# Two layers of attention and feed-forward on one core: score slots of three and two PSUM banks, with two banks shared by side work and single VectorE tiles

## The chip, the cores and the metric

The kernel runs on one core of one Trainium2 chip. The metric is the device time of the kernel in microseconds (us), from its first to its last instruction; the four executions of each kernel here lie within 0.4% of each other. The time before is 1714 us.

Names of engines: PE is TensorE (PEld its weight loads), ACT is ScalarE, DVE is VectorE, POOL is GpSimd, SP issues most transfers. PSUM is the memory in which TensorE leaves its results; it has eight banks, and one 128 x 512 fp32 result fills a bank.

## The reference

Two layers, each attention with 32 heads of width 16 over 2048 rows, then a gated feed-forward.

```python
def _A_ref(x, wqkv, wo):                 # x: 1 x 2048 x 512
    B, S, D = x.shape; H = 32; Dh = D // H
    qkv = ...(x @ wqkv)...               # cut: split into q, k, v by head
    scores = jnp.einsum("bhqd,bhkd->bhqk", q, k) * (Dh ** -0.5)
    p = _softmax(scores, axis=-1)
    o = jnp.einsum("bhqk,bhkd->bhqd", p, v)
    return ...(o)... @ wo
def _B_ref(x, w_gate, w_up, w_down):     # inner width 1792
    return (_gelu(x @ w_gate) * (x @ w_up)) @ w_down

x = A_x                                  # everything below twice, same weights
x = x + _A_ref(_layernorm(x), A_wqkv, A_wo)
x = x + _B_ref(_layernorm(x), B_w_gate, B_w_up, B_w_down)
```

Per layer there are 32 heads x 2048 x 2048 scores. In tiles of 128 keys x 512 queries that makes 2048 tiles a layer, 4096 in all. Each tile needs a matmul of contraction 16 (padded to 32 rows of the array), an exponential of every element, and a matmul with the values.

## The kernel before

The program is built by a list scheduler that runs while the kernel is being built. It keeps a clock of its own, decides the order of every engine's instructions, and emits a static program with semaphores. So a small edit of its rules changes the order of thousands of instructions.

The eight PSUM banks before: bank 7 collects attention outputs; banks 0 to 2 and 3 to 5 are two *slots* for scores; bank 6 is the only bank for *side work* (projections, the attention output projection, the feed-forward, transposes). A slot is filled by one burst of up to three score matmuls on different row groups of the array, and emptied by one ScalarE exponential.

```python
free_banks = set(range(7))               # 0-5 become the slots when scores start; 6 stays
...
def slot_banks():
    b0 = 3 * (slot_no[0] % 2)
    return [b0, b0 + 1, b0 + 2]
```

VectorE takes part of the exponentials. It adds a constant to the scaled score, clamps at zero and writes an int16, whose bits read as fp16 are about the exponential. Three further copies, shifted by quarters of an octave, are made on VectorE from a group of four such tiles, and the four variants are averaged by the value matmuls. In the kernel before, VectorE gets the *third* tile of a slot, and the choice is made for a group of 12 tiles (four slots) at once:

```python
size = 3 if m is not None and not pace["haste"] else 2
d = size == 3 and started_all() and vector_group() and behind() < LAG
for i in range(0, n, size):
    cur.append((layer, u, part, tiles, 4 * m + i // 3 if d else None, ...))
...
na = n - (dslot is not None)             # tiles that ScalarE takes from this slot: 2 or 3
o = sch.op("act", lambda e: e.activation(PT[...], PS[:, b0:b0 + na, :], ACTF.Exp, scale=...), ...)
...
slot_open[si] += 1                       # the slot can't be refilled before VectorE has drained it
dve(0, [(lambda e: e.tensor_scalar(PI[...], bank(b0 + n - 1), DBIAS, 0.0,
                                   op0=ALU.add, op1=ALU.max), ...)], then)
```

When TensorE would be idle for long, the scheduler inserts filler matmuls that add zero to bank 7. They are meant to keep TensorE's clock up. Near the end of a layer there is a hurried stretch ("haste"), in which scores go without VectorE and two banks of the slots are lent to side work.

## Time and profile before

| | before |
|---|---|
| median | 1714.07 us (1712.64 to 1716.61, 3 runs) |
| ScalarE busy | 1562 us, of it exponentials 1489 us |
| exponentials | 1092 of two banks, 348 of three |
| VectorE score tiles | 868 of 4096 |
| ScalarE idle before exponentials | 79 us |

From the page of the kernel before: its first line, the busy time of each engine, and the shares of the chain of waits by engine.

```profile
span 1715.0 us, 38081 instructions
...
PE 1614.4 (94%) x16017; PEld 489.6 (29%) x16017; DVE 1377.6 (80%) x2287; ACT 1562.4 (91%) x1486; POOL 201.0 (12%) x217
...
ACT 51%; PE 37%; DVE 9%; issue 1%; SPq 1%; DMA 1%; POOL 0%; DVEq 0%; POOLq 0%
```

ScalarE is at 91% over the whole span, and in the stretch with exponentials it is nearer 95%. The chain gives ScalarE half and TensorE over a third, so the two nearly tie.

The page's group of all exponentials. The numbers after the bar are the busy time in us and the mean of one in ns; then the idle time of ScalarE just before them, and what ended most of it.

```profile
L1149 ACT ACTIVATE fPT<-fPS 128x1024 bf16<-128x1024 f32 (+1 forms) x1440 | 1488.7, 1181 | 79.3 <-PE fPS L1144 76.9
```

So 1489 us are work and 79 us are waits for score matmuls. The groups of the kernel before with different shapes kept apart, in the same columns:

```profile
L1149 ACT ACTIVATE fPT<-fPS 128x1024 bf16<-128x1024 f32 x1092 | 1033.6, 1075 | 45.6 <-PE fPS L1144 43.9
L1183 DVE TENSOR_SCALAR fPI<-fPS 128x512 int16<-128x512 f32 x868 | 569.6, 682 | 92.2 <-PE fPS L1144 90.2
L1144 PE MATMUL fPS<-fQ,fKT 32*128 32x512 bf16 x4096 | 550.4, 386 | 62.4 <-ACT fPT L1149 45.1 <-DVE fPI L1183 5.2 <-DVE fQ L634 2.0
L1149 ACT ACTIVATE fPT<-fPS 128x1536 bf16<-128x1536 f32 x348 | 482.4, 1513 | 33.7 <-PE fPS L1144 33.1
L1274 PE MATMUL fPS<-fONB,fZV 128*17 128x512 bf16 x2724 | 212.0, 388 | 3.0 <-POOL fQMASK L361 1.5 <-DVE fOS L827 1.5
```

The first and fourth lines are the two kinds of exponentials, the second VectorE's score tiles, the third the score matmuls, the last the filler.

ScalarE's waits for score matmuls in four windows of the kernel before, in this order: 20 to 131 us, 131 to 790, 790 to 990 (around the layer boundary), 990 to 1680. The numbers are us in total, how many, and the longest.

```profile
ACT fPT L1149 <- PE fPS L1144: 17.1, 4, 6.6
ACT fPT L1149 <- PE fPS L1144: 17.6, 41, 1.9
ACT fPT L1149 <- PE fPS L1144: 20.1, 21, 11.4
ACT fPT L1149 <- PE fPS L1144: 18.2, 40, 1.7
```

With the 3.9 us before the first exponential these make the group's 76.9 us. In the first window it is four waits, in the third one of 11.4 us and twenty short ones; the other two consist of short waits only, 0.4 us on average. ScalarE's timeline of the kernel before, cut to the long gaps and the end (start in us, length, then the instructions; in brackets the idle time before):

```profile
17.39 12.21 ACT L1149 ACTIVATE fPT<-fPS 128x1536 bf16<-128x1536 f32 x9 [3.90 <-PE fPS L1144]
32.47 6.82 ACT L1149 ACTIVATE fPT<-fPS 128x1536 bf16<-128x1536 f32 x5 [2.87 <-PE fPS L1144]
41.44 31.87 ACT L1149 ACTIVATE fPT<-fPS 128x1536 bf16<-128x1536 f32 x30 [2.14 <-PE fPS L1144]
79.88 43.85 ACT L1149 ACTIVATE fPT<-fPS 128x1024 bf16<-128x1024 f32 x44 [6.58 <-PE fPS L1144]
129.26 1.45 ACT L1149 ACTIVATE fPT<-fPS 128x1536 bf16<-128x1536 f32 x1 [5.52 <-PE fPS L1144]
...
841.60 13.84 ACT L1149 ACTIVATE fPT<-fPS 128x1536 bf16<-128x1536 f32 x14 [11.35 <-PE fPS L1144]
...
1639.76 3.82 ACT L1149 ACTIVATE fPT<-fPS 128x1024 bf16<-128x1024 f32 x4 [0.68 <-PE fPS L1144]
1674.58 1.28 ACT L917 ACT_TABLE_LOAD   x1 [31.00 <-PE fPS L590]
```

From the last exponential's end (1639.76 + 3.82 = 1643.58 us) to the end of the span are 71.4 us, in which ScalarE has nearly nothing to do.

TensorE waits for VectorE's score tiles before score bursts, as matmul and as weight load (us in total, how many, and the longest):

```profile
PE fPS L1144 <- DVE fPI L1183: 5.2, 16, 0.9
PEld fPS L1144 <- DVE fPI L1183: 3.7, 10, 0.5
```

These 8.9 us are little.

### The profile page before, as it was taken

The page shows a single profiled execution, that of the slowest core. Times are in us where ns is not written, and L with a number is a line of the kernel's source. Part 1 is how long each engine was busy: PE and PEld are TensorE (multiplying, and loading weights), DVE is VectorE, ACT ScalarE, POOL GpSimd, SP SyncE. Part 2 cuts the span into 40 slices and gives each one's busy share as a digit, 9 for nine tenths or more (in the row PEclk, how much of TensorE's full clock was granted, in tenths as well). Part 3 has the DMA queues.
Part 4 walks back from the last instruction along what each step waited for, and adds up shares of the span by engine and source line. Part 5 has one row for each costly group of instructions (what it writes and reads, how often), then busy time and mean ns, then how long its engine had stood idle before and what let it go on. Part 6 is the DMA issues. An engine that isn't in the chain of part 4 may idle for free.

```text
span 1715.0 us, 38081 instructions
## 1 busy us (share of the span) xinstructions
PE 1614.4 (94%) x16017; PEld 489.6 (29%) x16017; DVE 1377.6 (80%) x2287; ACT 1562.4 (91%) x1486; POOL 201.0 (12%) x217
## 2 busy tenths in 40 slices
PE   8999989999999999999999999999999999999998
PEld 3333222222222222332333222222222222222233
DVE  7788868888898889878743878988888888887953
ACT  5889999999999999999699999999999999999932
POOL 2313011100211021000420110101011100201000
PEclk9999989999999999999999999999999999999999
DMA  4100000224202241125314000012330124112523
GB/s 136 51 2 18 2 18 20 53 76 141 51 27 56 88 145 37 40 53 160 92 47 145 26 18 10 16 40 59 118 110 26 54 70 142 49 38 61 151 59 107
DMA packets 140289, 111.88 MB, mean 65 GB/s; under 512 B 13904, under 2 KB 129872, under 8 KB 140112
## 3 DMA queue, kind: packets, MB, share of 16 engines
q1 hardware_dynamic: 136416, 104.78, 21.4%
q0 software_dynamic: 2112, 4.19, 0.9%
q8 instruction: 130, 2.13, 0.5%
q10 hardware_dynamic: 1584, 0.39, 0.1%
q14 instruction: 47, 0.39, 0.1%
HBM read 97.78 MB, written 6.82 MB: 61 GB/s over the span
## 4 chain that ended last, share of the span: by engine, by line
ACT 51%; PE 37%; DVE 9%; issue 1%; SPq 1%; DMA 1%; POOL 0%; DVEq 0%; POOLq 0%
ACT fPT L1149 50%; PE fPS L590 12%; PE fPS L1144 9%; PE fPS L1254 8%; PE fPS L1274 4%; DVE fPP L1205 4%; DVE fPI L1183 3%; PE fPS L951 2%; ACT fHT L1115 1%; PE fPS L654 1%; DVE fQ L634 1%; SPq L276 1%; DVE fHT L937 1%; PE fPS L567 0%; ACT L1115 0%
## 5 line engine op out<-in xcount | busy, mean ns | idle before, releaser
L1149 ACT ACTIVATE fPT<-fPS 128x1024 bf16<-128x1024 f32 (+1 forms) x1440 | 1488.7, 1181 | 79.3 <-PE fPS L1144 76.9
L1183 DVE TENSOR_SCALAR fPI<-fPS 128x512 int16<-128x512 f32 x868 | 569.6, 682 | 92.2 <-PE fPS L1144 90.2
L1144 PE MATMUL fPS<-fQ,fKT 32*128 32x512 bf16 x4096 | 550.4, 386 | 62.4 <-ACT fPT L1149 45.1
L1205 DVE TENSOR_SCALAR fPP<-fPI 128x2048 int16<-128x2048 int16 x651 | 442.2, 716 | 5.9 <-PE fPS L1254 3.7
L1254 PE MATMUL fPS<-fPT,fVP 128*17 128x512 bf16 x3228 | 438.2, 386 | 6.8 <-DVE fPP L1205 2.6
L1254 PE MATMUL fPS<-fPP,fVD 128*17 128x512 f16 x2604 | 334.1, 381 | 10.7 <-DVE fPP L1205 9.8
L1144 PEld LDWEIGHTS fPS<-fQ,fKT 32*128 32x128 bf16 x4096 | 139.0, 91 | 593.4 <-ACT fPT L1149 491.3
L1254 PE MATMUL fPS<-fPI,fVP 128*17 128x512 f16 x868 | 241.7, 385 | 1.7 <-DVE fPP L1205 1.6
L590 PE MATMUL fPS<-fXNT,fWR 128*128 128x512 bf16 x896 | 226.7, 381 | 5.3 <-DVE fHT L937 4.9
L1274 PE MATMUL fPS<-fONB,fZV 128*17 128x512 bf16 x2724 | 212.0, 388 | 3.0 <-POOL fQMASK L361 1.5
L1254 PEld LDWEIGHTS fPS<-fPT,fVP 128*17 128x17 f16 x3228 | 98.8, 87 | 162.4 <-issue 114.2
L937 DVE TENSOR_TENSOR fHT<-fPS,fHT 128x512 bf16<-128x512 f32 x112 | 76.7, 687 | 68.3 <-PE fPS L590 55.1
L786 POOL TENSOR_TENSOR fAT<-fOS,fRB 128x512 bf16<-128x512 f32 x32 | 42.3, 1322 | 715.9 <-DMA fRB<-rscr 567.4
L951 PE MATMUL fPS<-fWR,fHT 128*128 128x512 bf16 x448 | 123.4, 383 | 0.5 <-DVE fQ L634 0.4
L1254 PEld LDWEIGHTS fPS<-fPP,fVD 128*17 128x17 f16 x2604 | 78.8, 88 | 102.4 <-issue 43.4
L590 PEld LDWEIGHTS fPS<-fXNT,fWR 128*128 128x128 bf16 x896 | 71.9, 97 | 121.1 <-DVE fHT L937 21.2
L914 DVE CAST fHT<-fPS 128x512 bf16<-128x512 f32 x98 | 67.1, 686 | 39.7 <-PE fPS L590 39.7
L1274 PEld LDWEIGHTS fPS<-fONB,fZV 128*17 128x17 f16 x2724 | 61.7, 91 | 68.5 <-issue 33.0
L667 POOL TENSOR_SCALAR fVD<-fVP 128x544 f16<-128x544 f16 (+1 forms) x48 | 53.8, 1124 | 152.5 <-DVE fVP L675 149.9
L546 POOL TENSOR_SCALAR fLNS<-fMV 128x4 f32<-128x4 f32 (+1 forms) x17 | 5.8, 342 | 517.9 <-DVE fMV L539 517.9
L1254 PEld LDWEIGHTS fPS<-fPI,fVP 128*17 128x17 f16 x868 | 51.4, 87 | 40.6 <-issue 22.1
L827 DVE COPY fOS<-fPS 128x512 f32<-128x512 f32 x64 | 43.7, 682 | 15.1 <-PE fPS L1254 14.9
(60 smaller groups left out, 697.5 us busy)
## 6 DMA issues: line engine op xcount, KB each, us to landing
fWR<-in_B_w_down_dram SPq DMA_DIRECT2D x189, 256.0 KB, 3.0
fWR<-in_B_w_gate_dram SPq DMA_DIRECT2D x56, 256.0 KB, 3.3
fWR<-in_B_w_up_dram SPq DMA_DIRECT2D x56, 256.0 KB, 2.9
fRB<-rscr SPq DMA_DIRECT2D x256, 32.0 KB, 1.9
fX<-in_A_x_dram POOLq DMA_DIRECT2D x4, 1024.0 KB, 6.0
xscr<-fX SPq DMA_DIRECT2D x16, 256.0 KB, 2.6
fX<-xscr SPq DMA_DIRECT2D x4, 1024.0 KB, 6.0
fAT<-fATS SPq DMA_DIRECT2D x128, 16.0 KB, 1.8
```

The source lines that it names most:

```text
L590: ins = e.matmul(bank(bs[0])[:, 0:cols], lhsT=l, rhs=r_, start=(i == 0), stop=(i == n - 1))
L667: job("pool", 2, [(lambda e, dst=dst, src=src, ph=ph: e.tensor_scalar(dst, src, 2.0 ** (-ph / NPH), None, op0=ALU.mult), [("VP", c, k) for ...
L827: fn = lambda e: e.tensor_copy(OS[:, s, :], bank(ACC))
L914: evac_job(1, b, [(lambda e: e.tensor_copy(HT[:, ft, :], bank(b)), [BK[b]], [("HT", ft)], 0.6)], got(("gate", layer, qb, ft)))
L937: (lambda e: e.tensor_tensor(HT[:, ft, :], bank(b), HT[:, ft, :], op=ALU.mult), [BK[b], ("HT", ft)], [("HT", ft)], 0.62)], got(("up", laye ...
L951: ins = e.matmul(bank(b)[:, 0:D], lhsT=HT[:, ft, i * 128:(i + 1) * 128], rhs=WR[:, s, jj * D:(jj + 1) * D], start=(ft == 0), stop=(ft == N ...
L1144: ins = e.matmul(bank(b0 + k), lhsT=KT[32 * j:32 * j + 32, c, kt * 128:(kt + 1) * 128], rhs=Q[32 * j:32 * j + 32, qs, :], start=True, stop ...
L1149: o = sch.op("act", lambda e: e.activation(PT[:, p, 0:512 * na].rearrange("p (a b) -> p a b", a=na), PS[:, b0:b0 + na, :], ACTF.Exp, scale ...
L1183: dve(0, [(lambda e: e.tensor_scalar(PI[:, gi, 512 * r:512 * (r + 1)], bank(b0 + n - 1), DBIAS, 0.0, op0=ALU.add, op1=ALU.max), [bks[-1]], ...
L1205: shifts.append((s, [(lambda e: e.tensor_scalar(PP[:, s, :], PI[:, gi, :], int(OCT) * ph // NPH, None, op0=ALU.add), [("PI", gi, r) for r ...
L1254: ins = e.matmul(PS[32 * j:32 * j + VW, ACC, :], lhsT=l, rhs=r_, start=a, stop=z, tile_position=(0, 32 * j), skip_group_check=True)
L1274: ins = e.matmul(PS[32 * j:32 * j + VW, ACC, :], lhsT=ZV[:, :], rhs=ones, start=False, stop=False, tile_position=(0, 32 * j), skip_group_c ...
```

## The change

The intent: give side work and VectorE two banks in common, and let ScalarE have its slots alone. The slots become three banks (0 to 2) and two banks (3 and 4); banks 5 and 6 are shared. VectorE now takes single tiles, each in a shared bank, whenever its backlog allows, from the next few tiles in the queue. A burst may be held back until a shared bank comes free, as long as ScalarE has 0.45 us of work left. The normalised rows, Q, K and the attention rows become fp16 instead of bf16. The core of the diff, with cuts:

```diff
+    WAIT_D = 0.45
...
-    XNT = sb("fXNT", [128, NCK, S], BF)
-    KT = sb("fKT", [128, NCK, S], BF)
+    XNT = sb("fXNT", [128, NCK, S], F16)
+    KT = sb("fKT", [128, NCK, S], F16)
...                      # likewise Q, AT, ATS, the identity and the ones
+    SLOTS = ((0, 1, 2), (3, 4))
...
     def slot_banks():
-        b0 = 3 * (slot_no[0] % 2)
-        return [b0, b0 + 1, b0 + 2]
+        return list(SLOTS[slot_no[0] % 2])
...
+    def vector_bank():
+        if not free_banks:
+            return None
+        return min(free_banks, key=lambda b: (sch.ready("pe", w=[BK[b]]), b))
...
+    def pick(look=False):
+        cap = slot_cap()
+        want_d = not look and started_all() and behind() < LAG and vector_tile()
+        bd = vector_bank() if want_d else None
+        if bd is None or sch.ready("pe", w=[BK[bd]]) > now[0] + 0.02:
+            want_d = False
+        ...                # up to cap tiles for ScalarE and at most one for VectorE
...
+        if started_all() and not pace["haste"] and (free_banks or vb_busy):
+            free = min(...)                      # when the first shared bank comes free
+            if ready < free <= sch.free["act"] - WAIT_D:
+                ready = free
...
-    free_banks.update(range(6))
+    free_banks.update(range(5))
```

The shifted copies may now be made for fewer than four tiles where a unit ends. Smaller edits of the same diff: in the hurried stretch a burst may fill its whole slot (two tiles before) and one bank of a slot is lent instead of two, and value matmuls are also hurried when shifted copies wait for a buffer.

More of the change, by code (lines that the diff above doesn't have):

```diff
@@ L224, in _emit_fast @@
     HT = sb("fHT", [128, NFT, 512], BF)
-    IDN = sb("fIDN", [128, 128], BF)
-    ONB = sb("fONB", [128, 128], BF)
+    IDN = sb("fIDN", [128, 128], F16)
+    ONB = sb("fONB", [128, 128], F16)
     CM05 = sb("fCM05", [128, 4], F32)
@@ L236, in _emit_fast @@
     NQS = 6
-    Q = sb("fQ", [128, NQS, 512], BF)
+    Q = sb("fQ", [128, NQS, 512], F16)
     NOS = HB + 4
@@ L242, in _emit_fast @@
     RB = sb("fRB", [128, NRB, 512], F32)
-    AT = sb("fAT", [128, NCK, 512], BF)
-    ATS = sb("fATS", [128, 2, 512], BF)
+    AT = sb("fAT", [128, NCK, 512], F16)
+    ATS = sb("fATS", [128, 2, 512], F16)
     ST = sb("fST", [128, 8, 6], F32)
@@ L266, in bankbf @@
     def bankbf(b):
-        return PS[:, b, :].bitcast(BF)
+        return PS[:, b, :].bitcast(F16)
     wire = [0.0]
@@ L483, in give_back @@
             lent.discard(b)
-            slot_open[b // 3] -= 1
+            slot_open[0 if b in SLOTS[0] else 1] -= 1
         elif b in held3:
@@ L496, in piece_banks @@
                 if not slot_open[s]:
-                    pool_.update(range(3 * s, 3 * s + 3))
-        if pace["haste"] and slot_no[0] >= 2 and not returned[0]:
-            pool_.update(3 * s + 2 for s in range(2) if not slot_open[s])
+                    pool_.update(SLOTS[s])
+        if pace["haste"] and slot_no[0] >= 2 and not returned[0] and not slot_open[0]:
+            pool_.add(2)
         pool_ -= held3
@@ L515, in emit_piece @@
                     free_banks.discard(b)
-                elif b % 3 == 2 and pace["haste"]:
+                elif b == 2 and pace["haste"]:
                     held3.add(b)
                 else:
-                    slot_open[b // 3] += 1
+                    slot_open[0 if b in SLOTS[0] else 1] += 1
                     lent.add(b)
@@ L531, in xn @@
     def xn(i, alt):
-        return HT[:, i + 4 * alt, 0:D]
+        return HT[:, i + 4 * alt, 0:D].bitcast(F16)
     def xnkey(i, alt):
@@ L964, in post @@
                 if last:
-                    ob = XNT[:, i % NCK, 512 * qb + (i // NCK) * D:512 * qb + (i // NCK) * D + D]
+                    ob = XNT[:, i % NCK, 512 * qb + (i // NCK) * D:512 * qb + (i // NCK) * D + D].bitcast(BF)
                     def store(o, i=i, tt=tt, ob=ob):
@@ L1016, in _emit_fast @@
     DBIAS = OCT * (15.0 - LOG2_4M)
-    groups = []
+    segs = []
     for layer in range(n_rep):
         us = list(range(NU))
-        def unit(u, part, m0, m1, rest):
-            for m in range(m0, m1):
-                groups.append((layer, u, part, 12 * m, 12, m, m == m1 - 1 and not rest))
-            if rest:
-                groups.append((layer, u, part, 12 * m1, 4 * NKT - 12 * m1, None, True))
         if NQB > 1:
-            np_, m = (NPART, NMA) if layer else (2, 1)
+            np_, kts = (NPART, NKT - 4) if layer else (2, 4)
             for u in us[:np_]:
-                unit(u, "A", 0, m, False)
+                segs.append((layer, u, "A", 0, 4 * kts))
             for u in us[:np_]:
-                unit(u, "B", m, NM, 4 * NKT > 12 * NM)
+                segs.append((layer, u, "B", 4 * kts, 4 * NKT))
             us = us[np_:]
         for u in us:
-            unit(u, "F", 0, NM, 4 * NKT > 12 * NM)
+            segs.append((layer, u, "F", 0, 4 * NKT))
     cur = []
@@ L1042, in _emit_fast @@
     pt_no = [0]
-    dg_no = [0]
+    dg = {"n": 0, "items": [], "uk": None, "done": [0]}
     pp_no = [0]
@@ L1049, in _emit_fast @@
     started = {}
+    seg_left = {}
     closed = set()
@@ L1053, in slot_banks, with slot_cap, vector_tile @@
     def slot_banks():
-        b0 = 3 * (slot_no[0] % 2)
-        return [b0, b0 + 1, b0 + 2]
-    def vector_group():
-        if pend.get(("PI", dg_no[0] % NPI)):
+        return list(SLOTS[slot_no[0] % 2])
+    def slot_cap():
+        bs = slot_banks()
+        return len([b for b in bs if b not in held3])
+    def vector_tile():
+        if pace["haste"]:
+            return False
+        if not dg["items"] and pend.get(("PI", dg["n"] % NPI)):
             return False
@@ L1063, in vector_group @@
         return late < DVE_LATE
+    def vector_bank():
+        if not free_banks:
+            return None
+        return min(free_banks, key=lambda b: (sch.ready("pe", w=[BK[b]]), b))
+    vb_busy = {}
     def take_slot():
@@ L1068, in take_slot, with pull, tile_keys @@
         slot_no[0] += 1
+    def pick(look=False):
[4 more added lines that the diff above has]
+            want_d = False
+        a, d = [], None
+        for x in cur:
+            if len(a) == cap and (d is not None or not want_d):
+                break
+            t = x[3]
+            if want_d and d is None and t % 3 == 2 and t < 12 * NM and (not dg["items"] or dg["uk"] == x[:3]):
+                if len(a) == cap or all(y[3] % 4 != t % 4 for y in a):
+                    d = x
+                    continue
+            if len(a) < cap:
+                a.append(x)
+            elif x[3] > a[-1][3] + 3 or x[:3] != a[-1][:3]:
+                break
+        return a, d
+    def pull():
+        while len(cur) < 6 and nxt[0] < len(segs):
+            layer, u, part, t0, t1 = segs[nxt[0]]
+            if (layer, "q", u // 2) not in have or (layer, "k", (u % NG) // 2, t0 // 16) not in have:
+                break
+            nxt[0] += 1
+            uk = (layer, u, part)
+            seg_left[uk] = t1 - t0
+            cur.extend((layer, u, part, t) for t in range(t0, t1))
+    def tile_keys(x):
+        layer, u, part, t = x
+        c = (u % NG) // 2
+        return [("Q", (layer * NU + u) % NQS), ("KT", c, t // 16)]
     def fill_ready():
@@ L1076, in fill_ready @@
             return None
-        e = next_slot()
-        if e is None:
-            return None
-        layer, u, part, tiles, ds, _ = e
-        c = (u % NG) // 2
-        if (layer, "q", u // 2) not in have:
-            return None
-        for kb in {t // 16 for t in tiles}:
-            if (layer, "k", c, kb) not in have:
-                return None
-        if pend.get(("PT", pt_no[0] % NPT)) or len(tiles) == 3 and 3 * s + 2 in held3:
-            return None
-        return sch.ready("pe", [("Q", (layer * NU + u) % NQS)] + [("KT", c, kb) for kb in {t // 16 for t in tiles}],
-                         [BK[b] for b in slot_banks()[:len(tiles)]])
@@ L1092, in left @@
-    def left():
-        return cur or nxt[0] < len(groups)
-    def next_slot():
-        if not cur and nxt[0] < len(groups):
-            layer, u, part, t0, n, m, end = groups[nxt[0]]
-            if (layer, "q", u // 2) not in have or (layer, "k", (u % NG) // 2, t0 // 16) not in have:
-                return None
-            nxt[0] += 1
-            size = 3 if m is not None and not pace["haste"] else 2
-            d = size == 3 and started_all() and vector_group() and behind() < LAG
-            for i in range(0, n, size):
-                tiles = list(range(t0 + i, t0 + min(i + size, n)))
-                cur.append((layer, u, part, tiles, 4 * m + i // 3 if d else None, end and i + size >= n))
-        return cur[0] if cur else None
@@ L1108, in fill @@
-    def fill():
-        a_slot(cur.pop(0))
+        pull()
+        a, _ = pick(True)
+        a = [x for x in a if (x[0], "k", (x[1] % NG) // 2, x[3] // 16) in have]
+        if not a:
+            return None
+        if pend.get(("PT", pt_no[0] % NPT)):
+            return None
+        keys = []
+        for x in a:
+            keys += tile_keys(x)
+        ready = sch.ready("pe", keys, [BK[b] for b in slot_banks()[:len(a)]])
+        if started_all() and not pace["haste"] and (free_banks or vb_busy):
+            free = min([sch.ready("pe", w=[BK[b]]) for b in free_banks]
+                       + [max(sch.free["dve"], now[0]) + 0.75 for b in vb_busy])
+            if ready < free <= sch.free["act"] - WAIT_D:
+                ready = free
@@ L1111, in _emit_fast @@
+        return ready
+    def left():
+        return cur or nxt[0] < len(segs)
+    def fill():
+        a, d = pick()
+        ok = lambda x: (x[0], "k", (x[1] % NG) // 2, x[3] // 16) in have
+        a = [x for x in a if ok(x)]
+        if d is not None and not ok(d):
+            d = None
+        for x in a + ([d] if d is not None else []):
+            cur.remove(x)
+        a_slot(a, d)
     table = {"gelu": False}
@@ L1118, in gelus, with enter @@
         have.add(("gelu", layer, qb))
-    def a_slot(entry):
-        layer, u, part, tiles, dslot, end = entry
-        tiles_filled[0] += len(tiles)
-        uk = (layer, u, part)
-        b0 = slot_banks()[0]
-        si = slot_no[0] % 2
-        take_slot()
-        g = u % NG
-        c, par = g // 2, g % 2
-        qs = (layer * NU + u) % NQS
-        p = pt_no[0] % NPT
-        pt_no[0] += 1
-        n = len(tiles)
-        na = n - (dslot is not None)
-        bks = [BK[b0 + k] for k in range(n)]
+    def enter(x):
+        uk = x[:3]
         if uk not in unit_q:
@@ L1139, in a_slot @@
             unit_order.append(uk)
+        seg_left[uk] -= 1
+        if not seg_left[uk]:
+            closed.add(uk)
+            if uk[2] != "A":
+                filled_units[0] += 1
+    def a_slot(atiles, dtile):
+        both = atiles + ([dtile] if dtile is not None else [])
+        tiles_filled[0] += len(both)
+        bd = vector_bank() if dtile is not None else None
+        banks = slot_banks()[:len(atiles)] + ([bd] if dtile is not None else [])
+        b0 = banks[0]
+        take_slot()
+        p = pt_no[0] % NPT
+        pt_no[0] += 1
+        na = len(atiles)
+        for x in both:
+            enter(x)
@@ L1141, in fn @@
         def fn(e):
-            for k, t in enumerate(tiles):
+            for b, (layer, u, part, t) in zip(banks, both):
                 kt, j = t // 4, t % 4
-                ins = e.matmul(bank(b0 + k), lhsT=KT[32 * j:32 * j + 32, c, kt * 128:(kt + 1) * 128],
-                               rhs=Q[32 * j:32 * j + 32, qs, :], start=True, stop=True, tile_position=(32 * j, 0))
-            return ins
-        pe(fn, [("Q", qs)] + [("KT", c, kb) for kb in sorted({t // 16 for t in tiles})], bks, MM, "row")
+                ins = e.matmul(bank(b), lhsT=KT[32 * j:32 * j + 32, (u % NG) // 2, kt * 128:(kt + 1) * 128],
+                               rhs=Q[32 * j:32 * j + 32, (layer * NU + u) % NQS, :], start=True, stop=True,
+                               tile_position=(32 * j, 0))
@@ L1149, in a_slot @@
+            return ins
+        keys = []
+        for x in both:
+            for k in tile_keys(x):
+                if k not in keys:
+                    keys.append(k)
+        js = [x[3] % 4 for x in both]
+        pe(fn, keys, [BK[b] for b in banks], MM * max(js.count(j) for j in js), "row")
+        bks = [BK[b] for b in banks[:na]]
         o = sch.op("act", lambda e: e.activation(PT[:, p, 0:512 * na].rearrange("p (a b) -> p a b", a=na),
                                                  PS[:, b0:b0 + na, :], ACTF.Exp, scale=1.0 / (OCT * LOG2E)),
-                   r=bks[:na], w=[("PT", p)], cost=0.049 + 0.427 * na + (1.3 if table["gelu"] else 0), lat=0.16)
+                   r=bks, w=[("PT", p)], cost=0.049 + 0.427 * na + (1.3 if table["gelu"] else 0), lat=0.16)
@@ L1152, in a_slot, with add @@
         table["gelu"] = False
-        def add(t, j, lhs, rhs, rk, needs, buf):
-            unit_q[uk].append((t, j, lhs, rhs, rk, needs, buf))
-            pend[buf] = pend.get(buf, 0) + 1
-        for k in range(na):
-            kt, j = tiles[k] // 4, tiles[k] % 4
-            add(o.seen, j, VP[:, c, par, 4 * kt + j, :], PT[:, p, 512 * k:512 * (k + 1)],
-                [("PT", p), ("VP", c, kt // 4), ("VPONE",)], (layer, "v", c, kt // 4), ("PT", p))
-        if dslot is not None:
-            m, r = dslot // 4, dslot % 4
-            gi = dg_no[0] % NPI
-            kt, j = tiles[-1] // 4, tiles[-1] % 4
-            assert tiles[-1] == 3 * dslot + 2 and j == D_J[r]
-            slot_open[si] += 1
+        def add(x, t, rhs, rk, buf):
+            layer, u, part, tt = x
+            kt, j = tt // 4, tt % 4
+            c, par = (u % NG) // 2, (u % NG) % 2
+            unit_q[x[:3]].append((t, j, VP[:, c, par, 4 * kt + j, :], rhs,
+                                  rk + [("VP", c, kt // 4), ("VPONE",)], (layer, "v", c, kt // 4), buf))
+            pend[buf] = pend.get(buf, 0) + 1
@@ L1168, in a_slot @@
+        for k, x in enumerate(atiles):
+            add(x, o.seen, PT[:, p, 512 * k:512 * (k + 1)], [("PT", p)], ("PT", p))
+        if dtile is not None:
+            uk = dtile[:3]
+            gi = dg["n"] % NPI
+            r = len(dg["items"])
+            if not r:
+                dg["done"] = [0]
+            done, items = dg["done"], dg["items"]
+            items.append(dtile)
+            dg["uk"] = uk
+            free_banks.discard(bd)
+            vb_busy[bd] = True
             unit_left[uk] += NPH
-            pend[("PI", gi)] = pend.get(("PI", gi), 0) + 1
@@ L1170, in a_slot @@
-            if r == 3:
-                dg_no[0] += 1
-                pend[("PI", gi)] += NPH - 1
+            pend[("PI", gi)] = pend.get(("PI", gi), 0) + NPH
             def then(o):
-                slot_open[si] -= 1
+                del vb_busy[bd]
+                free_banks.add(bd)
                 unit_left[uk] -= 1
                 pend[("PI", gi)] -= 1
-                add(o.seen, j, VP[:, c, par, 4 * kt + j, :], PI[:, gi, 512 * r:512 * (r + 1)].bitcast(F16),
-                    [("PI", gi, r), ("VP", c, kt // 4), ("VPONE",)], (layer, "v", c, kt // 4), ("PI", gi))
-                if r == 3:
-                    for ph in range(1, NPH):
-                        shift(uk, c, g, m, gi, ph)
@@ L1183, in a_slot @@
-            dve(0, [(lambda e: e.tensor_scalar(PI[:, gi, 512 * r:512 * (r + 1)], bank(b0 + n - 1), DBIAS, 0.0,
-                                               op0=ALU.add, op1=ALU.max), [bks[-1]], [("PI", gi, r)], 0.6)], then)
-        if end:
-            closed.add(uk)
-            if part != "A":
-                filled_units[0] += 1
-    def shift(uk, c, g, m, gi, ph):
-        layer = uk[0]
-        vd = "A" if m < NMA else "B"
+                add(dtile, o.seen, PI[:, gi, 512 * r:512 * (r + 1)].bitcast(F16), [("PI", gi, r)], ("PI", gi))
@@ new lines, in then, with ripe @@
+                done[0] += 1
+                ripe(items, gi, done)
+            dve(0, [(lambda e: e.tensor_scalar(PI[:, gi, 512 * r:512 * (r + 1)], bank(bd), DBIAS, 0.0,
+                                               op0=ALU.add, op1=ALU.max), [BK[bd]], [("PI", gi, r)], 0.6)], then)
+        if dg["items"] and (len(dg["items"]) == 4 or seg_left[dg["uk"]] < 4 and not any(
+                x[:3] == dg["uk"] and x[3] % 3 == 2 and x[3] < 12 * NM for x in cur)):
+            flush()
+    def ripe(items, gi, done):
+        if dg["items"] is not items and done[0] == len(items):
+            for ph in range(1, NPH):
+                shift(items, gi, ph)
@@ L1193, in shift, with flush @@
+    def flush():
+        items, gi, done = dg["items"], dg["n"] % NPI, dg["done"]
+        dg["n"] += 1
+        dg["items"] = []
+        ripe(items, gi, done)
+    def shift(items, gi, ph):
         s = pp_no[0] % NPS
         pp_no[0] += 1
+        n = len(items)
+        uk = items[0][:3]
+        layer, u, _ = uk
+        c, g = (u % NG) // 2, u % NG
         def then(o):
-            pend[("PI", gi)] -= 1
-            for r in range(4):
+            pend[("PI", gi)] -= n
+            for r, x in enumerate(items):
+                i = x[3] // 3
+                vd = "A" if i < 4 * NMA else "B"
@@ L1199, in then @@
                 unit_left[uk] -= 1
-                unit_q[uk].append((o.seen, D_J[r], VD[:, c, ph - 1, g % 2, 4 * m + r, :],
+                unit_q[uk].append((o.seen, x[3] % 4, VD[:, c, ph - 1, g % 2, i, :],
                                    PP[:, s, 512 * r:512 * (r + 1)].bitcast(F16),
@@ L1203, in then @@
                 pend["PP", s] = pend.get(("PP", s), 0) + 1
-        shifts.append((s, [(lambda e: e.tensor_scalar(PP[:, s, :], PI[:, gi, :], int(OCT) * ph // NPH, None,
-                                                      op0=ALU.add),
-                            [("PI", gi, r) for r in range(4)], [("PP", s)], 2.8 if ph in POOLED else 0.6)], then, ph in POOLED))
+        shifts.append((s, [(lambda e: e.tensor_scalar(PP[:, s, 0:512 * n], PI[:, gi, 0:512 * n], int(OCT) * ph // NPH,
+                                                      None, op0=ALU.add),
+                            [("PI", gi, r) for r in range(n)], [("PP", s)], 0.067 + 0.1333 * n)], then, False))
     shifts = []
-    POOLED = ()
     def feed_shifts():
@@ L1404, in _emit_fast @@
                 full = max(byj)
-        press = F is None and left() and pend.get(("PT", pt_no[0] % NPT))
+        press = F is None and left() and pend.get(("PT", pt_no[0] % NPT)) or shifts and pend.get(("PP", shifts[0][0]))
         if press and its:
             full = max(full, 1)
-        want = 1 if pend.get(("PI", dg_no[0] % NPI)) else 3
+        want = 1 if pend.get(("PI", dg["n"] % NPI)) and not dg["items"] else 3
         if fit >= 1 and (full >= want or full and (rest or press)):
```

## The prediction

> **What bounds the kernel now.** ScalarE's exponentials. The page's busy table gives ScalarE 1562 us of 1715 (91%), TensorE 1614, VectorE 1378. From the first exponential (17.4 us) to the last (1643.6 us, ScalarE's timeline) ScalarE is idle only some 75 us: the exponentials' group has 79 us of idle before it, nearly all for score matmuls. Before 17.4 us and after 1643.6 us (71 us of last feed-forward) the change does nothing. VectorE is busy about 87% in a middle slice. TensorE is nearly critical: the chain of waits puts 51% on ScalarE, 37% on TensorE; but 212 us of its busy time is clock-keeping filler.
>
> **What stays.** In the built programs, exponentials go from 1092 of two banks and 348 of three to 649 and 651 (and two of one); VectorE's share of 4096 score tiles falls from 868 to 843. The groups' means (1075 and 1513 ns) give 438 ns a tile, which leaves 52 ns fixed per instruction: 3228 x 0.438 + 1440 x 0.052 = 1489 us. After, an estimate: 3253 x 0.438 + 1302 x 0.052 = 1493 us, +4 us. The Trainium skill, "ScalarE: Activation LUTs" (What ACT_TABLE_LOAD costs), has the same form, a fixed part plus 0.833 ns an element; the trace has 0.855. VectorE saves some 21 us, not critical. fp16 for bf16 changes no width, and mixed bf16 x fp16 matmuls already run here at 386 ns against 381 for fp16 alone: I expect nothing from it.
>
> **What moves.** All gain is ScalarE idle. By window its waits are 21 us up to 130 us (three gaps of 6.6, 5.5 and 2.1 us, in which TensorE runs K, V and Q projections that the next scores need, one side bank at a time), 23 us to 810, 20 us at the layer boundary (one gap of 11.4), 18 us after it. With two side banks projections come earlier: 60 of the first layer's 64 K matmuls lie within the first 256 score tiles, before 44. Score bursts fall from 1440 to about 1302; one takes 0.39 us with three tiles or four, so TensorE gains some 50 us of slack. The time to refill a slot alternates between 0.93 and 1.37 us instead of being mostly 0.93. I expect the early gaps to lose 12 us, the boundary 4, the many 0.3 us waits 15 of 41: minus 31, plus 4.
>
> **Against it.** A burst with a VectorE tile takes a shared bank planned to be free just then, and may be held until shortly before ScalarE runs dry; its waits all stand before its first matmul. A late VectorE drain (682 ns each) thus delays ScalarE's tiles too. Before, that bank had a whole further slot's time to drain.
>
> **Prediction.** 1687 us, 1658 to 1716 in 8 of 10. Faster by over 2%: 0.37; within: 0.55; slower: 0.08.
>
> **What would show each step.** Exponentials' busy time 1488 to 1500 us; their idle falling from 79 to about 48 us; the gaps at 73 and 124 us gone or halved; the last 71 us unchanged; filler falling from 2724 to 2452 matmuls; matmul means still 380 to 390 ns. Wrong if score matmuls' waits for VectorE's score tiles (9 us now, weight loads included) grow to tens of us, or if the granted clock (0.99) falls as filler goes.
>
> **What would make it wrong.** Upwards: VectorE lateness as above. Downwards: short waits nearly all gone, 1660; the floor, no middle idle, is about 1643 us.

## More of the kernel before

The timeline of all engines, cut to TensorE's matmuls and ScalarE, in the later part of the gap that ends at 79.88 us:

```profile
75.16 1.03 PE L590 MATMUL fPS<-fXNT,fWK 128*128 128x512 bf16 x4
76.02 1.06 PE L654 MATMUL fPS<-fWV,fXNT 128*128 128x128 bf16 x16
76.92 1.03 PE L590 MATMUL fPS<-fXNT,fWQ 128*128 128x512 bf16 x4
77.78 1.03 PE L590 MATMUL fPS<-fXNT,fWK 128*128 128x512 bf16 x4
79.44 0.39 PE L1144 MATMUL fPS<-fQ,fKT 32*128 32x512 bf16 x3 [0.64 <-DVE fQ L634]
79.88 2.86 ACT L1149 ACTIVATE fPT<-fPS 128x1024 bf16<-128x1024 f32 x3 [6.58 <-PE fPS L1144]
```

TensorE is busy nearly throughout with V, K and Q projections, because the next unit's scores need this Q and these K. The work is not wasted, it comes too late. Inside such a gap side work has more than one bank, because the scheduler then lends it the banks of idle slots: V's matmuls start at 76.02 us, before VectorE begins to copy K's result out at 76.22 us. It is before the gap that side work has one bank.

## The result, and the profile after

| | before | after |
|---|---|---|
| median | 1714.73 us (4 runs) | 1683.82 us (1683.13 to 1684.63, 4 runs) |
| ratio of fast runs | | 0.9821, interval 0.9807 to 0.9835 |
| exponentials, busy | 1488.7 us | 1487.9 us |
| idle before exponentials | 79.3 us | 46.3 us |
| the rest of the span | 147.0 us | 148.7 us |
| granted TensorE clock | 0.994 | 0.999 |

A ratio is worked out from the fast runs of the same rounds, so it is not quite the ratio of the medians. The change is faster by 1.8%; the interval excludes no change, and also a gain of 2%. The three rows before the last split the span of the profiled execution: 1488.7 + 79.3 + 147.0 = 1715.0 and 1487.9 + 46.3 + 148.7 = 1682.9. All of the gain is idle time of ScalarE.

From the page of the changed kernel, the same lines:

```profile
span 1682.9 us, 37093 instructions
...
PE 1576.2 (94%) x15611; PEld 492.6 (29%) x15670; DVE 1378.6 (82%) x2334; ACT 1561.6 (93%) x1348; POOL 203.4 (12%) x217
...
ACT 52%; PE 35%; DVE 10%; DMA 1%; issue 1%; SPq 1%; POOL 0%; POOLq 0%; DVEq 0%
```

The group of all exponentials after, and then the groups with shapes kept apart (exponentials, VectorE's score tiles, score matmuls, filler):

```profile
L1204 ACT ACTIVATE fPT<-fPS 128x1536 bf16<-128x1536 f32 (+1 forms) x1302 | 1487.9, 1284 | 46.3 <-PE fPS L1191 42.5
```

```profile
L1204 ACT ACTIVATE fPT<-fPS 128x1536 bf16<-128x1536 f32 x651 | 974.3, 1497 | 36.3 <-PE fPS L1191 34.0
L1204 ACT ACTIVATE fPT<-fPS 128x1024 bf16<-128x1024 f32 x649 | 696.6, 1073 | 10.0 <-PE fPS L1191 8.5
L1241 DVE TENSOR_SCALAR fPI<-fPS 128x512 int16<-128x512 f32 x843 | 571.0, 684 | 93.4 <-PE fPS L1191 87.6
L1191 PE MATMUL fPS<-fQ,fKT 32*128 32x512 f16 x4096 | 513.2, 384 | 50.0 <-ACT fPT L1204 36.3 <-DVE fPI L1241 3.6 <-DVE fHT L916 1.6
L1344 PE MATMUL fPS<-fONB,fZV 128*17 128x512 f16 x2452 | 189.6, 385 | 2.3 <-POOL fQMASK L362 1.5 <-DVE fOS L829 0.8
```

The exponentials are fewer and longer, but their busy time is the same. The means of the matmuls are nearly as before, 384 and 385 ns against 386 and 388. The score matmuls' busy time fell from 550 to 513 us, as there are fewer bursts. VectorE's busy time did not fall, although it has 25 tiles fewer.

ScalarE's waits for score matmuls after, in the same four windows in the same order:

```profile
ACT fPT L1204 <- PE fPS L1191: 6.6, 2, 5.3
ACT fPT L1204 <- PE fPS L1191: 13.5, 32, 1.1
ACT fPT L1204 <- PE fPS L1191: 7.7, 9, 4.8
ACT fPT L1204 <- PE fPS L1191: 10.8, 27, 1.2
```

The differences are 10.5, 4.1, 12.4 and 7.4 us. Together they are 34.4 us of the 76.9. ScalarE's timeline after, with the gaps that are left and the end:

```profile
17.67 28.57 ACT L1204 ACTIVATE fPT<-fPS 128x1536 bf16<-128x1536 f32 x25 [3.90 <-PE fPS L1191]
47.52 23.20 ACT L1204 ACTIVATE fPT<-fPS 128x1024 bf16<-128x1024 f32 x21 [1.28 <-PE fPS L1191]
76.06 65.37 ACT L1204 ACTIVATE fPT<-fPS 128x1536 bf16<-128x1536 f32 x57 [5.34 <-PE fPS L1191]
...
821.87 5.54 ACT L1204 ACTIVATE fPT<-fPS 128x1024 bf16<-128x1024 f32 x5 [4.79 <-PE fPS L1191]
828.48 9.39 ACT L1204 ACTIVATE fPT<-fPS 128x1536 bf16<-128x1536 f32 x8 [1.07 <-PE fPS L1191]
...
1589.19 20.95 ACT L1204 ACTIVATE fPT<-fPS 128x1024 bf16<-128x1024 f32 x19
1641.22 1.28 ACT L919 ACT_TABLE_LOAD   x1 [31.08 <-PE fPS L592]
```

The early gaps went from four to two. The gap at 124 us is gone, the one at 73 us is still there, at 5.3 us. The layer boundary has 4.8 us instead of 11.4. The last exponential ends at 1589.19 + 20.95 = 1610.14 us, which leaves 72.8 us of end, 1.4 us more than before. Score bursts' waits for VectorE's tiles after:

```profile
PEld fPS L1191 <- DVE fPI L1241: 11.8, 36, 0.4
PE fPS L1191 <- DVE fPI L1241: 3.6, 11, 0.5
```

They rose from 8.9 to 15.4 us, not to tens of us.

### The profile page after: what moved, and what is told of

It reads as the page before. It is cut to its first block, busy times and chain, and to the rows that moved or that the text cites. A ratio compares the mean times of both kernels' runs of the same rounds, so it can differ in the third digit from the quotient of the medians.

```text
span 1682.9 us, 37093 instructions
## 1 busy us (share of the span) xinstructions
PE 1576.2 (94%) x15611; PEld 492.6 (29%) x15670; DVE 1378.6 (82%) x2334; ACT 1561.6 (93%) x1348; POOL 203.4 (12%) x217
## 4 chain that ended last, share of the span: by engine, by line
ACT 52%; PE 35%; DVE 10%; DMA 1%; issue 1%; SPq 1%; POOL 0%; POOLq 0%; DVEq 0%
ACT fPT L1204 49%; PE fPS L592 11%; PE fPS L1324 9%; PE fPS L1191 9%; DVE fPP L1277 4%; PE fPS L953 4%; DVE fPI L1241 3%; ACT fHT L1157 2%; PE fPS L1344 2%; DVE fHT L939 1%; SPq L277 1%; DVE fHT L916 1%; ACT L1157 1%; PE fPS L656 1%; DVE fQ L636 0%
## 5 line engine op out<-in xcount | busy, mean ns | idle before, releaser
L1204 ACT ACTIVATE fPT<-fPS 128x1536 bf16<-128x1536 f32 (+1 forms) x1302 | 1487.9, 1284 | 46.3 <-PE fPS L1191 42.5
L1241 DVE TENSOR_SCALAR fPI<-fPS 128x512 int16<-128x512 f32 x843 | 571.0, 684 | 93.4 <-PE fPS L1191 87.6
L1191 PE MATMUL fPS<-fQ,fKT 32*128 32x512 f16 x4096 | 513.2, 384 | 50.0 <-ACT fPT L1204 36.3
L1324 PE MATMUL fPS<-fPT,fVP 128*17 128x512 bf16 x3253 | 469.0, 382 | 11.7 <-DVE fOS L829 5.6
L1277 DVE TENSOR_SCALAR fPP<-fPI 128x2048 int16<-128x2048 int16 (+3 forms) x723 | 444.7, 645 | 8.1 <-PE fPS L1324 2.3
L1324 PE MATMUL fPS<-fPP,fVD 128*17 128x512 f16 x2529 | 409.7, 381 | 10.8 <-DVE fPP L1277 5.9
L1191 PEld LDWEIGHTS fPS<-fQ,fKT 32*128 32x128 f16 x4096 | 129.0, 91 | 533.7 <-ACT fPT L1204 382.4
L592 PE MATMUL fPS<-fXNT,fWR 128*128 128x512 f16 x896 | 221.7, 381 | 10.4 <-DVE fHT L939 6.0
L1344 PE MATMUL fPS<-fONB,fZV 128*17 128x512 f16 x2452 | 189.6, 385 | 2.3 <-POOL fQMASK L362 1.5
L788 POOL TENSOR_TENSOR fAT<-fOS,fRB 128x512 f16<-128x512 f32 x32 | 41.3, 1291 | 817.2 <-DMA fRB<-rscr 791.6
L592 PEld LDWEIGHTS fPS<-fXNT,fWR 128*128 128x128 bf16 x896 | 72.8, 98 | 128.3 <-DVE fHT L939 19.6
L788 POOL TENSOR_TENSOR fATS<-fOS,fRB 128x512 f16<-128x512 f32 x32 | 42.3, 1323 | 78.2 <-DMA fRB<-rscr 78.2
```

Of the source, the lines that this page charges most:

```text
L592: ins = e.matmul(bank(bs[0])[:, 0:cols], lhsT=l, rhs=r_, start=(i == 0), stop=(i == n - 1))
L788: job("pool", 1, [(lambda e: e.tensor_tensor(dst, OS[:, os_, :], RB[:, slot, :], op=ALU.mult), [("OS", os_)] + [("RB", slot, j) for j in r ...
L1191: ins = e.matmul(bank(b), lhsT=KT[32 * j:32 * j + 32, (u % NG) // 2, kt * 128:(kt + 1) * 128], rhs=Q[32 * j:32 * j + 32, (layer * NU + u) ...
L1204: o = sch.op("act", lambda e: e.activation(PT[:, p, 0:512 * na].rearrange("p (a b) -> p a b", a=na), PS[:, b0:b0 + na, :], ACTF.Exp, scale ...
L1241: dve(0, [(lambda e: e.tensor_scalar(PI[:, gi, 512 * r:512 * (r + 1)], bank(bd), DBIAS, 0.0, op0=ALU.add, op1=ALU.max), [BK[bd]], [("PI", ...
L1277: shifts.append((s, [(lambda e: e.tensor_scalar(PP[:, s, 0:512 * n], PI[:, gi, 0:512 * n], int(OCT) * ph // NPH, None, op0=ALU.add), [("PI ...
```

## The experiments

My theory was that ScalarE's work stays the same and that its idle time falls because side work and VectorE have two banks in common. The rivals were fp16, the longer exponentials by themselves, and later VectorE's lateness. All experiments but the first replan the whole program, so each differs from its neighbour in more than its edit. What I compare is therefore work and idle separately. "Rest" is the span less the exponentials' busy time and the idle before them.

| kernel | VectorE tiles | exponentials | busy us | idle us | rest us | median us | ratio to before |
|---|---|---|---|---|---|---|---|
| before | 868 | 1440 | 1488.7 | 79.3 | 147.0 | 1714.7 | 1 |
| the change | 843 | 1302 | 1487.9 | 46.3 | 148.7 | 1683.8 | 0.9821 |
| e1 fp16 alone | 868 | 1440 | 1488.1 | 77.7 | 147.2 | 1714.0 | 1.0000 |
| e2 no hold | 781 | 1327 | 1511.4 | 33.4 | 145.9 | 1692.6 | 0.9882 |
| e3 one shared bank | 517 | 1435 | 1636.8 | 109.9 | 152.1 | 1902.1 | 1.1104 |
| e5 slots 2 and 2 | 988 | 1555 | 1452.0 | 122.4 | 147.2 | 1725.4 | 1.0073 |
| e6 side work on one bank | 806 | 1318 | 1504.2 | 68.9 | 155.8 | 1730.9 | 1.0101 |
| e7 VectorE tiles on one bank | 648 | 1380 | 1573.0 | 30.2 | 149.0 | 1752.6 | 1.0222 |
| e8 shorter hold, more tiles | 868 | 1292 | 1480.7 | 69.9 | 148.4 | 1698.9 | 0.9909 |
| e9 more tiles | 882 | 1286 | 1474.3 | 73.7 | 149.2 | 1697.1 | 0.9894 |
| e10 slots 2 and 2, fewer tiles | 849 | 1624 | 1511.9 | 90.0 | 147.3 | 1751.7 | 1.0233 |
| e11 earlier pace, more tiles | 854 | 1298 | 1486.2 | 60.3 | 147.2 | 1694.7 | 0.9888 |
| e12 before, fewer tiles | 720 | 1440 | 1549.8 | 57.5 | 145.8 | 1754.9 | 1.0247 |

### e1: fp16 alone

The edit is the fp16 part of the diff above on the kernel before, with the order of instructions unchanged.

> The kernel before with only the fp16 tensors of the change; same order of instructions (1092 and 348 exponentials, 868 VectorE tiles). Theory (the banks made the gain): 1714 us, ratio to before 0.998 to 1.002, matmul means 380 to 390 ns, ScalarE idle before exponentials still near 79 us. Rival (fp16 made some of it, by faster matmuls, evictions or a better granted clock): 1684 to 1705 us.

Measured: 1714.03 us, ratio 1.0000 (0.9984 to 1.0017). The group of exponentials of e1:

```profile
L1149 ACT ACTIVATE fPT<-fPS 128x1024 bf16<-128x1024 f32 (+1 forms) x1440 | 1488.1, 1181 | 77.7 <-PE fPS L1144 75.6
```

Nothing moved. The clock in the profiled run was 0.998, against 0.994 in that of before, and the time was the same, so the clock is not the source of the gain either.

### e2: no hold

```diff
-    WAIT_D = 0.45
+    WAIT_D = 1e9
```

> The changed kernel, but a score burst is never held back for a VectorE bank to come free. The built program has 781 VectorE tiles instead of 843, so ScalarE does 3315 tiles in 1327 instructions: 3315 x 0.438 + 1327 x 0.052 = 1521 us, 28 us more than my figure for the changed kernel. Theory (the hold buys VectorE tiles and costs little idle): 1700 to 1715 us, exponentials busy about 1516 us, idle before them 35 to 50 us. Rival (the hold starves ScalarE, and its late bursts are the idle that is left): idle falls below 30 us, and time is 1690 us or less.

Measured: 1692.62 us, which is faster than I had expected, and neither story was whole. Work rose by 23.5 us, as the theory had it. But the idle also fell by 12.9 us, below my 35 to 50, though not below the rival's 30. The hold buys 62 VectorE tiles and pays for them with ScalarE idle; the balance is about 9 us in its favour.

### e3: one shared bank

```diff
-    free_banks = set(range(7))
+    free_banks = {0, 1, 2, 3, 4, 6}
```

> The changed kernel with one of its two shared banks left unused (slots of three and two banks as in the change). The built program has only 517 VectorE tiles: ScalarE does 3579 tiles in 1435 instructions, an estimate of 1642 us. Theory (the second shared bank carries the gain): 1820 to 1880 us, exponentials busy about 1637 us, the early gaps of over 2 us back (15 us or more up to 130 us). Rival (the three-bank and two-bank slots and the finer choice of tiles carry it, the shared bank only helps): under 1714 us.

Measured: 1902.11 us, slower than my range. The exponentials' busy time was as expected (1636.8), the early window had 25.9 us of waits, and the idle was 109.9 us. Score bursts' waits for VectorE's tiles in e3:

```profile
PEld fPS L1191 <- DVE fPI L1241: 60.6, 146, 2.1
PE fPS L1191 <- DVE fPI L1241: 25.5, 68, 1.8
```

These are 86 us, against 15 in the change. The coupling that I feared in the prediction is real, and it takes the second shared bank to keep it small. In this scheduler the new slots and the finer choice of tiles are worth nothing without it: its plan gave VectorE only 517 tiles.

### e5 and e10: slots of two and two banks, three shared banks

```diff
-    SLOTS = ((0, 1, 2), (3, 4))
+    SLOTS = ((0, 1), (2, 3))
-    free_banks.update(range(5))
+    free_banks.update(range(4))
...                      # no bank of a slot is lent in the hurried stretch
```

> The changed kernel with slots of two and two banks and three shared banks. The built program has 988 VectorE tiles, and 1553 two-bank exponentials (two of one): 3108 x 0.438 + 1555 x 0.052 = 1442 us, 50 us under the changed kernel; VectorE would have about 145 x (0.68 + 0.53) = 175 us more, 1554 us. Theory (shared banks set how much VectorE can take, and ScalarE is the limit): faster than the change, 1645 to 1675 us, VectorE 93 to 95% busy, idle before exponentials up to 70 to 90 us as VectorE becomes a second limit. Rival (longer exponentials, which leave TensorE a longer time to refill, carry the gain): 1690 to 1730 us, with more than 110 us of idle.

Measured: 1725.38 us with 122.4 us of idle. Here my theory fell and the rival was right in both of its numbers. VectorE was 88% busy over the span, though, so it could have been full. The next run took VectorE's load away, with the backlog limit cut to 1.0 us (`DVE_LATE = 1.0`).

> The kernel with slots of two and two and three shared banks again, with VectorE's backlog limit cut from 2.0 to 1.0 us, which brings its VectorE tiles down from 988 to 849, about those of the change (843). Estimate of exponentials: 3247 x 0.438 + 1624 x 0.052 = 1507 us, so about 1502 us busy. In all runs so far the time is exponentials' busy time, plus idle before them, plus 146 to 156 us. Theory (two-bank slots starved ScalarE because VectorE was full, 988 tiles): idle falls from 122 to 35 to 55 us, 1685 to 1705 us. Rival (two-bank exponentials are too short for TensorE to refill the slot behind its other work): idle stays above 85 us, 1735 us or more.

Measured: 1751.71 us. The group of exponentials of e10:

```profile
L1204 ACT ACTIVATE fPT<-fPS 128x1024 bf16<-128x1024 f32 x1624 | 1511.9, 1084 | 90.0 <-PE fPS L1191 86.8
```

At the change's number of VectorE tiles the idle is 90.0 us, not 46. The waits outside the first window and the layer boundary are 58.2 us (32.8 and 25.4), against 24.3 in the change and 35.8 before. Even the early window has 15.3 us, with three banks shared. So the third bank of a slot is worth having. Two reasons fit and are not separated here: an exponential of two banks can be over before TensorE is through with its other work and can refill, and the 1624 bursts (1302 in the change) take more of TensorE's time (the score matmuls' group is 618.7 us against 513.2). Of the 32 us that e5 lost in idle against e10, VectorE's load may be the cause. Most of the rest goes with the slots.

### e6 and e7: which use of the second bank pays

e6 takes the second shared bank from side work, outside the hurried stretch:

```diff
         pool_ -= held3
+        if slot_no[0] >= 2 and not pace["haste"] and not returned[0]:
+            pool_.discard(5)
```

> The changed kernel, but side work may use only one of the two shared banks (outside the hurried stretch at the end of a layer, where it keeps both); VectorE tiles may use both. The built program has 806 VectorE tiles, an estimate of 1510 us of exponentials (17 us more than my figure for the change, so about 1504 us busy). Theory (the second bank pays through projections and feed-forward pieces that come in time): gaps of 15 us or more up to 131 us again (6.6 us in the changed kernel), idle before exponentials 60 to 75 us, 1710 to 1730 us. Rival (the second bank pays only through VectorE tiles): idle stays at 40 to 50 us, 1695 to 1704 us.

Measured: 1730.93 us, slightly above my range, with 68.9 us of idle. Against the change that is 22.6 us more idle, 16.3 us more work and 7.1 us more of the rest. The early window has 13.7 us of waits (6.6 in the change), a little under my 15, and the window of the layer boundary 28.2 us (7.7 in the change). The short waits did not rise (19.4 us, against 24.3). K projections from 17.4 to 72 us, that is up to about the gap, in the kernel before, the change and e6 (window, length, then busy us and count of matmuls and of weight loads; the rest of a line is the clock and DMA):

```profile
17.40:72.00 54.60, 5.17 (x20) 1.56 (x20) 0.97 0.22 57
17.40:72.00 54.60, 7.26 (x28) 2.16 (x28) 1.00 0.21 56
17.40:72.00 54.60, 5.18 (x20) 1.55 (x20) 1.00 0.22 58
```

The V projections' matmuls there are 67, 112 and 70. So with two banks side work gets further in the same time, and with one bank it is back where it was before. ScalarE's timeline of e6, the ends of its two longest gaps:

```profile
82.56 22.72 ACT L1206 ACTIVATE fPT<-fPS 128x1536 bf16<-128x1536 f32 x20 [8.95 <-PE fPS L1193]
...
860.29 4.73 ACT L1206 ACTIVATE fPT<-fPS 128x1536 bf16<-128x1536 f32 x4 [25.14 <-PE fPS L1193]
```

In the boundary gap the chain is this: the last residual sum of the last but one block, its layernorm, transposes, K and V projections, then the second layer's first scores. The last residual sum of that block ran on VectorE at 827.9 us before, at 805.2 us in the change, and at 848.4 us in e6. The scores behind it reached ScalarE at 841.6, 821.9 and 860.3 us. Side work that gets its banks late ends late, and the next layer starts late.

e7 takes the second shared bank from VectorE's tiles:

```diff
-        if not free_banks:
+        mine = free_banks & {5}
+        if not mine:
             return None
-        return min(free_banks, key=...)
+        return min(mine, key=...)
```

> The changed kernel, but VectorE tiles may use only one of the two shared banks; side work may use both. The built program has 648 VectorE tiles, an estimate of 1582 us of exponentials, so about 1576 us busy, 88 us more than in the change. Theory (both uses of the second bank count, and ScalarE's work goes up tile by tile where VectorE gets less): 1765 to 1800 us, early gaps as in the change (10 us or less). Rival (VectorE tiles are not what the shared banks buy): under 1715 us.

Measured: 1752.59 us, below my range. Work rose as expected to 1573.0 us, but the idle fell to 30.2 us, which I had not expected. The early window has 3.3 us and the boundary 1.8 us. So both uses of the bank count. They pull in different directions, as far as these two runs show: more VectorE tiles mean less work for ScalarE and more waits.

### e8, e9 and e11: can more VectorE tiles beat the change?

e8: `WAIT_D = 0.55`, `DVE_LATE = 3.0`. e9: `DVE_LATE = 3.0`. e11: `DVE_LATE = 2.5` and

```diff
-        f = (... - NG * (posts_done[0] + 1) - 1.0) / (NG - 1.5)
+        early = 2.5 if posts_done[0] % NQB == NQB - 2 else 1.5
+        f = (... - NG * (posts_done[0] + 1) - 1.0) / (NG - early)
```

> The changed kernel with the hold shortened (0.55 us ahead of ScalarE running dry instead of 0.45) and more VectorE backlog allowed (3.0 us instead of 2.0). The built program has 868 VectorE tiles: an estimate of 1481 us of exponentials, 12 us less. Theory (the hold's late bursts are idle; VectorE, 82% busy, has room for 25 tiles more): exponentials busy about 1476 us, idle 35 to 45 us, 1662 to 1676 us. Rival (VectorE's lateness is already what leaves ScalarE idle): idle over 55 us, 1684 us or more.

> The changed kernel with only the VectorE backlog limit raised (3.0 us instead of 2.0), the hold as in the change. The built program has 882 VectorE tiles: an estimate of 1475 us of exponentials, 18 us less. Theory (ScalarE's work decides, the hold keeps its idle where it was): busy about 1470 us, idle 44 to 56 us, 1664 to 1678 us. Rival (VectorE's lateness): idle over 64 us, 1684 us or more.

> The changed kernel with two small edits: the feed-forward pieces of the last but one block of a layer are paced to end one unit of attention earlier, and VectorE's backlog limit is 2.5 us. The built program has 854 VectorE tiles, an estimate of 1487 us of exponentials (6 us less than for the change). Theory (the gap at the layer boundary waits for a chain of VectorE and side work that ends late, and goes when that starts earlier): waits between 790 and 990 us 4 us or less (7.7 in the change, 20.8 with the limit at 3.0), idle 38 to 48 us, 1668 to 1680 us. Rival (the gap is set by VectorE's share of tiles alone): 8 to 15 us there, 1684 us or more.

Measured: 1698.92, 1697.14 and 1694.66 us; all are slower than the change, and all three are misses of my theory. The rival's figures were met each time. In e9 work fell by 13.6 us and idle rose by 27.4. VectorE's share over the span was 83%, so it was not full on average, and score bursts waited for its tiles 13.7 us, no more than in the change. So it was not the direct stall of score bursts. The waits that grew in e9 are in the middle of the first layer (22.9 us, from 13.5) and at the boundary (20.8 us, one of 15.6, from 7.7). In e11 the boundary has 9.3 us, so pacing that block earlier did not close the gap; there is no run with the limit at 2.5 us alone, so what the pacing did by itself is not known.

The traces hold an indirect path that I had overlooked. Side work now shares its banks with VectorE's tiles and waits for them too. The waits of the projections' and feed-forward's matmuls and weight loads (line 592; line 590 in the kernel before; V's are another line) for VectorE's score tiles are 2.0 us before and 29.9 us in the change. Among the kernels with the change's banks they are 21.6 us at 781 VectorE tiles (e2), 29.9 at 843, 42.3 at 854 (e11), 45.8 at 868 (e8) and 41.6 at 882 (e9). That goes roughly with the idle, but it is not a test.

### e12: the kernel before with fewer VectorE tiles

`DVE_LATE = 1.0` in the kernel before. Its output was judged wrong by a hair (relative error 0.0200033).

> The kernel before with VectorE's backlog limit cut from 2.0 to 1.0 us: 720 VectorE tiles instead of 868, an estimate of 1554 us of exponentials. Theory (the kernel before is idle because its side work has one bank, not because VectorE is late): idle stays at 60 to 80 us, early gaps 13 us or more up to 131 us, 1755 to 1780 us. Rival (the idle of before came of VectorE's load, as it does in the change with more tiles): idle 25 to 40 us, 1725 to 1742 us.

Measured: 1754.89 us and 57.5 us of idle, just outside the theory's figures and far from the rival's. The early window keeps 16.1 us of waits (17.1 before). The boundary falls from 20.1 to 13.0 us, and the short waits from 35.8 to 21.1. So with one bank for side work the early gaps stay even with 148 VectorE tiles fewer, while a part of the boundary and of the short waits did come of VectorE's load.

## Why the prediction was right

The prediction of 1687 us came within 3.2 us of 1683.8. Its main mechanism is what the profile and e6 show: idle of ScalarE goes because side work comes earlier. That the total came so near is in part luck, because terms were missed in both directions: in the profiled spans the layer boundary gave 8.4 us more than forecast and the work 4.8 us more, the short waits 3.5 us less, the early gaps 1.5 us less, and the rest and other idle 3.1 us less. The terms one by one:

- **"All gain is ScalarE idle."** Right. Idle before exponentials fell from 79.3 to 46.3 us (predicted: about 48), and everything else moved by 1 us net.
- **"+4 us" of exponentials.** Mis-sized: it was -0.8 us. I split the cost by the difference of the two means, 438 ns a tile and 52 ns an instruction. The busy times of the twelve kernels with different counts, fitted by least squares, give 422 ns a tile and 89 ns an instruction, with all residuals under 5 us. With those numbers, 25 tiles more cost 10.5 us and 138 instructions fewer save 12.3 us, so the work stays. The means contain time in which one exponential overlaps the next (1075 ns for two banks, where the fit has 933), and can't be split so. The Trainium skill, "ScalarE: Activation LUTs" (What ACT_TABLE_LOAD costs), has 186 ns fixed with 93 ns of overlap, which leaves 93 ns, and 0.833 ns an element, which is 427 ns for 512: within 5% of the fit. I had quoted the page and then trusted the means against it.
- **The early gaps "lose 12 us".** They lost 10.5. I had listed three gaps; the trace has a fourth, of 2.87 us before 32.47 us. "One side bank at a time" was right for the time before the gaps and wrong inside them (see the timeline above). e6 brings most of the loss back by taking one bank from side work, and e12 shows that lighter VectorE work does not remove it. The Trainium skill, "Perfetto Trace Analysis" (Optimizing Tensor Performance), says that independent matmul groups should rotate through different PSUM banks so that the evacuation of one overlaps the next; these traces agree. Before, V's matmuls start at 46.43 us, after K's result has been copied out of the one bank (45.68 to 46.37 us); in the change V's start at 45.24 us, before that copy starts (45.44 us). With the change's slots the early waits are 13.7 us with one bank for side work (e6) and 6.6 us with two. Banks for side work are not all of it, as e10 has three and 15.3 us.
- **The layer boundary loses "4".** Mis-sized: it lost 12.4. I had not followed the chain there: feed-forward, layernorm, K projection, scores. That chain is side work: its last residual sum moved from 827.9 to 805.2 us, and the scores behind it from 841.6 to 821.9 us.
- **The short waits lose "15 of 41".** The 41 was a wrong reading. I had added two windows whose border, at 130 us, fell into the exponential that ended the gap at 124 to 129 us (129.26 to 130.71 us), and so counted its 5.5 us twice. The short waits were 35.8 us and lost 11.5.
- **"TensorE gains some 50 us of slack."** Mis-sized: the score matmuls' group shrank by 37 us. TensorE's whole busy time fell by 38 us, while the filler's group fell by 22.
- **"VectorE saves some 21 us."** Wrong, at no cost: its busy time went from 1377.6 to 1378.6 us. The score tiles take 571.0 us for 843, against 569.6 for 868, and the shifted copies 444.7 against 442.2, now in 723 instructions instead of 651.
- **fp16: "nothing".** Right (e1, ratio 1.0000).
- **"Against it".** The coupling exists (86 us of waits in e3), but with two shared banks it stayed at 15.4 us for score bursts. The prediction did not have the second path, side work that waits for VectorE's tiles (29.9 us in the change, 2.0 before). The clock did not fall with less filler (2452 matmuls, as counted): 0.994 to 0.999.

What the prediction had not asked is whether more VectorE tiles would pay. In the kernels tried they do not, though e2, e8 and e11 differ from the change in more than the count. Among kernels with its slots and both banks for all, idle is 33.4 us at 781 VectorE tiles, 46.3 at 843, 60.3 at 854, 69.9 at 868 and 73.7 at 882, while busy time falls by about 0.37 us a tile from 781 to 882 ((1511.4 - 1474.3) / 101). Work plus idle is 1544.8, 1534.2, 1546.5, 1550.6 and 1548.0 us, least in the change.

Two things stay open. The short waits fell by 11.5 us, and e10 shows that slots of two banks have many more of them, but I did not separate longer exponentials from the finer choice of tiles. And why idle grows so fast beyond 843 tiles is not settled: it is not the direct stall of bursts on VectorE's tiles; side work's waits for them grow too, but no run tests that; and since each of these programs is planned anew, a part may be chance of the plan.

## What to carry to other kernels

When one engine is the limit and nearly full, write its time as work plus waits, and predict the two apart: here the work did not change by 1 us, and the whole gain was waits. Give PSUM banks out by what arrives late: here a second bank for work beside the main loop was worth more than a sixth bank for the scores, but slots of two banks each gave it all back. And when the border of two windows falls into the instruction that ended a wait, the wait is counted in both, so check that the windows add up to the group's total.

## What the Trainium skill lacked or had wrong

- "ScalarE: Activation LUTs" (What ACT_TABLE_LOAD costs) gives 1283 ns for a table load and about 1380 ns for a drain, 2.66 us for every switch. In these traces the load agrees: the 14 loads around the gelus took 1283 ns on average. The drain does not show: in the changed kernel the exponentials end at 872.97 us, the load runs from 872.99 to 874.27 us, and the gelu starts at 874.29 us.
- "TensorEngine Tiling (Array Packing)" (PSUM Bottleneck) advises to use ScalarE and VectorE both to empty PSUM. No page says what that costs in banks: with one bank shared by VectorE's tiles and side work the time was 1902 us (517 VectorE tiles), with two 1684 us (843).
- "Perfetto Trace Analysis" (Optimization Strategy) says that consistent bubbles on the engine that should be saturated can mean too little PSUM. The early gaps here came of too few banks too (13.7 us in e6, 6.6 in the change), but they are few and long (four up to 131 us before, the longest 6.6 us), not one repeating bubble. The section names too little PSUM for the repeating kind alone.
